# Reordering loads and DMA transposes on the queues of a four-batch attention and MLP-mixer kernel

## The chip, the cores and the metric

One core of a Trainium2 chip. The metric is the device time of one execution in microseconds (us); several executions are timed and the median is quoted. A profile is one more execution, taken by the hardware profiler. Its span is a little shorter than the timed figure of the same execution (256.6 against 258.4 us before).

The engines, as this kernel uses them: PE does the matrix products, ACT the functions such as Exp and Relu, DVE and POOL element-wise work, and SP here only issues DMA transfers (PEld is the loading of weights for PE). PSUM is where this kernel has PE put its results; an eviction is the copy of such a tile out of PSUM by ACT or DVE. The granted clock is the share of PE's full clock that it got (1.00 is full).

## The reference, cut to what matters

Four batches, eight heads, 768 positions, head dimension 64. Each query sees its window of 128 keys and the first four keys (the sinks). The attention output, as `[batch, 768, 512]`, goes through an MLP mixer.

```python
def _attn_ref(q, k, v, n_sink, window):
    scores = scale * np.matmul(q, k.transpose(0, 1, 3, 2))
    keep = is_sink | in_window              # 4 sinks, window of 128
    a = softmax(np.where(keep, scores, -1e9))       # written out in the original
    return np.matmul(a, v)

def _moe_ref(x, w_tok1, w_tok2, w_ch1, w_ch2):
    xt = x.transpose(0, 2, 1)
    h = np.maximum(xt @ w_tok1, 0.0) @ w_tok2
    u = x + h.transpose(0, 2, 1)            # token mixing
    h2 = np.maximum(u @ w_ch1, 0.0) @ w_ch2 # channel mixing
    return u + h2
```

## The kernel before

Batches run one behind the other, overlapped: while the channel layers of batch b run on PE, the attention of batch b+1 is threaded in between, and near the end the token layers of batch b+1 (its "head"). The heads of a batch form two groups of four; groups 2 and 3 belong to batch 1, 4 and 5 to batch 2, 6 and 7 to batch 3. The program order is also the order on each engine's queue: a `spread` function places each piece of the fill at a fraction of the main work.

Names used below: `x_b` is the attention output, `u` (`u_sb`) the token-mixing result, `uT` its transpose (for batches 1 to 3 by DMA transposes, six per batch, issued from the SP queue), `ps_v` the PSUM tile of the first channel layer (24 tiles a batch, evicted in turn by ACT and DVE), `ps_w` that of the second. The seam is the place where PE goes from the last `ps_w` of one batch to the first `ps_v` of the next. It needs the first three `uT`.

```python
def cast_and_turn(G, which, copy):              # q (0) or k (1) of a group
    ...
    copy(...)                                   # float32 to bf16, on POOL
    nc.sync.dma_start_transpose(out=T, in_=flat)

def utr(st):                                    # one of six transposes of u
    if b > 0:
        nc.sync.dma_start_transpose(out=uT[:, :, ts(st, P)], in_=u_sb[:, st])
        return
    ...                                         # batch 0: by PE and ACT

def ch1(half, ft):                              # first channel layer, one tile
    ...
    if ft % 2 == 0:
        nc.scalar.activation(v1[...], ps, AF.Relu)
    else:
        nc.vector.tensor_scalar(out=v1[...], in0=ps, scalar1=0.0, scalar2=None, op0=ALU.max)

def prep_v(g):
    cast_v(held[g])
    if g + 2 < NG and g >= 2:
        fetch(g + 2)                            # three loads of 768 KB from SP: q, k, v
...
seq += [build_mask0, lambda: cast_sinks(GB, NG)]   # last of the start: DVE and POOL work
run(seq)
for b in range(B):
    main, fill = mixers.pop(b)[2], []
    ...                                         # attention of batch b+1: up to fraction mid
    if b + 2 < B:
        fill += [(mid + 0.01, lambda n=n: prep_qk(n)) for n in (h + 1, h + 2)]
        fill += [(mid + 0.01, lambda n=n: prep_v(n)) for n in (h + 1, h + 2)]
    hi = mid + 0.03                             # then the head: token layers, transposes of u
    fill += [(hi + (0.97 - hi) * n / (len(nhead) - 1), f) for n, (f, _) in enumerate(nhead)]
    run(spread(main, fill))
```

The softmax here doesn't subtract the row's maximum and nothing guards it: scores larger than these inputs give would overflow.

## Time and profile before

Median 257.99 us of three runs (256.86 to 258.50). The two lines below, from the profile page of the kernel before, give 40 equal slices of the span (6.4 us each): the busy tenths of PE, and the granted PE clock in tenths of full speed.

```profile
PE   8996859997998960005888999979799999999993
PEclk9999968999999997555999999997999999999999
```

PE is nearly always busy, but for a hole in slices 16 to 18. The clock is lower at the hole (0.7 and then 0.5 in slices 16 to 19), once near 35 us (0.6) and once near 174 us (0.7). The stretches below put numbers on the stages from the first `ps_v` of batch 0 (37.48 us). The columns are the stretch, its length, busy us and instructions for each engine, the clock, the DMA share (which in this view can come out above 1, here up to 1.28, and serves to compare) and GB/s.

```profile
core 0: us, PE busy (x) PEld busy (x) DVE busy (x) ACT busy (x) POOL busy (x), PEclk, DMA share, GB/s
37.48:94.00 56.52, 53.16 (x413) 29.43 (x417) 29.43 (x65) 25.05 (x39) 29.56 (x35) 0.97 1.02 207
94.00:118.53 24.53, 0.00 (x0) 0.03 (x1) 0.66 (x1) 0.00 (x0) 0.00 (x0) 0.60 1.28 222
118.53:168.21 49.68, 47.41 (x348) 25.69 (x353) 20.85 (x47) 20.32 (x38) 23.65 (x28) 0.96 0.38 81
168.21:218.77 50.56, 47.04 (x349) 25.59 (x352) 21.54 (x48) 20.60 (x38) 15.06 (x20) 0.97 0.17 49
```

Batch 0, the hole, batch 1 and batch 2. In the hole no engine computes, and DMA has the highest share of the four (1.28). Who waited for whom, on PE (us in total, times, longest):

```profile
PE ps_v L350 <- DMA uT<-u_sb: 24.6, 1, 24.6
PE ps_v L350 <- ACT v_1341 L353: 3.3, 3, 1.9
PE ps_v L350 <- ACT v_584 L353: 2.1, 3, 0.7
```

One wait for a transpose of u is 24.6 us. Its cause is on the SP queue, shown here in order of time (start, duration of the issue, line, what):

```profile
89.36 1.64 SPq L122 DMA_TRANSPOSE kT<-kb  x1
91.06 0.98 SPq L103 DMA_DIRECT2D q_1248<-in_q_dram  x1
92.09 2.54 SPq L103 DMA_DIRECT2D k_1249<-in_k_dram  x1
94.73 3.47 SPq L135 DMA_DIRECT2D v_1252<-in_v_dram  x1
...
105.50 3.50 SPq L135 DMA_DIRECT2D v_1263<-in_v_dram  x1
109.09 3.46 SPq L371 DMA_DIRECT2D out_dram<-o  x1
112.64 2.52 SPq L340 DMA_TRANSPOSE uT<-u_sb  x2
```

Six loads of batch 3, of which four are shown, stand ahead of the transposes of u, and behind them an output store of 3.5 us. At 67.5 us, more than 7 us after SP's last issue, a load took SP 0.37 us to issue; here, one behind the other, four of the six took about 3.5 us each. An estimate from the trace sets this beside the data: 768 KB at 218 GB/s (slices 16 and 17 of the page) take 3.6 us, so SP issued about as fast as the data moved. The last u had been ready on DVE since 92.9 us.

### The profile page before, as it was taken

The page shows a single profiled execution, that of the slowest core. Times are in us where ns is not written, and L with a number is a line of the kernel's source. Part 1 is how long each engine was busy: PE and PEld are TensorE (multiplying, and loading weights), DVE is VectorE, ACT ScalarE, POOL GpSimd, SP SyncE. Part 2 cuts the span into 40 slices and gives each one's busy share as a digit, 9 for nine tenths or more (in the row PEclk, how much of TensorE's full clock was granted, in tenths as well). Part 3 has the DMA queues.
Part 4 walks back from the last instruction along what each step waited for, and adds up shares of the span by engine and source line. Part 5 has one row for each costly group of instructions (what it writes and reads, how often), then busy time and mean ns, then how long its engine had stood idle before and what let it go on. Part 6 is the DMA issues. An engine that isn't in the chain of part 4 may idle for free.

```text
span 256.6 us, 3888 instructions
## 1 busy us (share of the span) xinstructions
PE 210.2 (82%) x1547; PEld 112.7 (44%) x1565; DVE 107.0 (42%) x241; ACT 91.1 (36%) x152; POOL 91.1 (36%) x121
## 2 busy tenths in 40 slices
PE   8996859997998960005888999979799999999993
PEld 3444624554565520002445665434456644554441
DVE  5657644364746450000225473531344636333221
ACT  3794224469751000002775421065754200231100
POOL 8759322018999300000485980015654000000000
PEclk9999968999999997555999999997999999999999
DMA  6999999599499999997100149550001115401122
GB/s 231 320 195 178 233 293 260 183 210 228 94 216 229 241 212 218 218 231 160 43 0 3 41 96 191 147 143 0 3 0 43 41 43 135 111 0 43 41 82 82
DMA packets 82113, 34.88 MB, mean 136 GB/s; under 512 B 72544, under 2 KB 78432, under 8 KB 82096
## 3 DMA queue, kind: packets, MB, share of 16 engines
q1 hardware_dynamic: 76560, 26.22, 49.1%
q0 software_dynamic: 4576, 7.11, 12.6%
q10 hardware_dynamic: 960, 1.31, 1.5%
q8 instruction: 12, 0.20, 0.3%
q14 instruction: 5, 0.04, 0.1%
HBM read 26.77 MB, written 6.29 MB: 129 GB/s over the span
## 4 chain that ended last, share of the span: by engine, by line
PE 57%; SPq 12%; ACT 10%; DVE 8%; DMA 6%; POOL 3%; issue 2%; DVEq 0%; ACTq 0%; POOLq 0%
PE ps_v L350 20%; PE ps_w L362 18%; ACT pT L248 7%; SPq L103 4%; DMA v_948<-in_v_dram 4%; PE ps_s L242 3%; PE ps_u L335 3%; SPq L135 3%; PE ps_h L328 3%; DMA uT<-u_sb 2%; PE ps_warm L468 2%; SPq L122 2%; SPq L371 2%; PE ps_tr L211 2%; SPq L340 2%
## 5 line engine op out<-in xcount | busy, mean ns | idle before, releaser
L350 PE MATMUL ps_v<-uT,w_ch_104 128*128 128x384 bf16 x384 | 77.6, 338 | 31.1 <-DMA uT<-u_sb 24.6
L350 PEld LDWEIGHTS <-w_ch_104 128*128 128x128 bf16 x384 | 36.6, 100 | 62.8 <-issue 42.9
L248 ACT ACTIVATE pT<-ps_s 128x1024 bf16<-128x1024 f32 (+1 forms) x48 | 43.6, 957 | 8.5 <-PE ps_s L242 7.8
L252 POOL TENSOR_TENSOR pT<-pT,mask_92 128x512 bf16<-128x512 bf16 x12 | 13.8, 1153 | 74.8 <-ACT pT L248 74.8
L365 DVE TENSOR_TENSOR o<-ps_w,u_sb 128x512 f32<-128x512 f32 x24 | 16.6, 692 | 22.0 <-PE ps_w L362 22.0
L336 DVE TENSOR_TENSOR u_sb<-ps_u,x_b 128x512 bf16<-128x512 f32 x24 | 16.3, 687 | 18.3 <-PE ps_u L335 17.0
L259 POOL TENSOR_SCALAR_AFFINE_SELECT pT<-pT 128x640 bf16<-128x640 bf16 x24 | 18.3, 764 | 13.8 <-ACT pT L248 13.8
L355 DVE TENSOR_SCALAR v_584<-ps_v 128x384 bf16<-128x384 f32 x12 | 6.7, 557 | 38.9 <-PE ps_v L350 38.9
L353 ACT ACTIVATE v_584<-ps_v 128x384 bf16<-128x384 f32 x12 | 5.9, 494 | 42.7 <-PE ps_v L350 42.6
L293 DVE TENSOR_TENSOR x_b<-ps_o,rc 128x256 bf16<-128x256 f32 x42 | 17.8, 425 | 1.5
L362 PE MATMUL ps_w<-w_ch_105,v_584 128*128 128x512 bf16 x69 | 17.5, 379 | 0.2
L362 PE MATMUL ps_w<-w_ch_105,v_1341 128*128 128x512 bf16 x69 | 17.5, 379 | 0.2
L362 PE MATMUL ps_w<-w_ch_105,v_112 128*128 128x512 bf16 x68 | 17.3, 379 | 0.2
L242 PE MATMUL ps_s<-qT,kT 64*128 64x256 bf16 x192 | 16.0, 275 | 1.3 <-ACT pT L248 0.8
L353 ACT ACTIVATE v_1922<-ps_v 128x384 bf16<-128x384 f32 x12 | 5.9, 491 | 29.7 <-PE ps_v L350 16.2
L362 PE MATMUL ps_w<-w_ch_105,v_1922 128*128 128x512 bf16 x70 | 15.9, 379 | 0.1
L262 POOL TENSOR_SCALAR_AFFINE_SELECT pT<-pT 128x512 bf16<-128x512 bf16 x24 | 15.6, 650 | 0.0
L280 PEld LDWEIGHTS <-pT 128*128 128x128 bf16 x192 | 14.3, 98 | 2.8 <-issue 0.4
L280 PE MATMUL ps_o<-va,pT 128*128 128x65 bf16 x168 | 14.9, 194 | 0.0
L292 DVE RECIPROCAL rc<-ps_o 128x4 f32<-128x4 f32 x42 | 7.5, 179 | 17.1 <-PE ps_o L284 10.5
L328 PE MATMUL ps_h<-x_b,w_tok_102 128*128 128x256 bf16 x96 | 13.4, 272 | 1.0 <-DVE x_b L293 0.5
L353 ACT ACTIVATE v_1341<-ps_v 128x384 bf16<-128x384 f32 x12 | 5.9, 493 | 22.3 <-DVE o L365 13.4
(130 smaller groups left out, 271.6 us busy)
## 6 DMA issues: line engine op xcount, KB each, us to landing
out_dram<-o SPq DMA_DIRECT2D x23, 256.0 KB, 2.2
w_ch_104<-in_moe_w_ch_dram POOLq DMA_DIRECT2D x2, 768.0 KB, 9.3
w_ch_105<-in_moe_w_ch_dram POOLq DMA_DIRECT2D x2, 768.0 KB, 18.8
k_114<-in_k_dram ACTq DMA_DIRECT2D x2, 384.0 KB, 5.6
q_113<-in_q_dram SPq DMA_DIRECT2D x2, 384.0 KB, 4.9
q_119<-in_q_dram SPq DMA_DIRECT2D x2, 384.0 KB, 8.3
v_117<-in_v_dram SPq DMA_DIRECT2D x1, 768.0 KB, 10.6
v_123<-in_v_dram SPq DMA_DIRECT2D x1, 768.0 KB, 13.7
```

The lines of the kernel that those rows point to most:

```text
L242: nc.tensor.matmul(ps[:, i, at:at + w].rearrange("p (c q) -> p c q", q=P), G.T[1][j][ds(64 * i, 64), kt], G.T[0][j][ds(64 * i, 64), kt:kt ...
L248: nc.scalar.activation(pT[:, :, 512 * u:512 * u + n], ps[:, :, 0:n], AF.Exp, scale=scale)
L259: nc.gpsimd.affine_select(out=cur, in_=cur, compare_op=ALU.is_ge, fill=0.0, base=0, pattern=[[0, NT - 1], [1, P]], channel_multiplier=-1)
L262: nc.gpsimd.affine_select(out=prv, in_=prv, compare_op=ALU.is_ge, fill=0.0, base=-1, pattern=[[0, NT - 2], [-1, P]], channel_multiplier=1)
L280: nc.tensor.matmul(o, pT[:, i, ds(256 * qt, P)], G.va[:, h, qt], start=(qt < 2 and h == 0), stop=(h == GH - 1 and qt == 0), skip_group_che ...
L293: nc.vector.tensor_tensor(out=x_b[:, qt, c0:c0 + GH * D].rearrange("p (h d) -> p h d", h=GH), in0=o[:, :, 0:D], in1=rc.to_broadcast([P, GH ...
L328: nc.tensor.matmul(ps, w_tok1[:, t, ts(tt, P)], x_b[:, t, ds(a * GH * D, GH * D)], start=(t == 0), stop=(t == NT - 1))
L336: nc.vector.tensor_tensor(out=u_sb[:, st], in0=ps, in1=x_b[:, st], op=ALU.add)
L350: nc.tensor.matmul(ps, w_ch1[:, c, ts(ft, P)], uT[:, c, ds(half * HS, HS)], start=(c == 0), stop=(c == NC - 1))
L353: nc.scalar.activation(v1[:, ft, ds(half * HS, HS)], ps, AF.Relu)
L362: nc.tensor.matmul(ps, v1[:, ft, ts(st, P)], w_ch2[:, ft], start=(ft == 0), stop=(ft == NF - 1))
L365: nc.vector.tensor_tensor(out=o, in0=ps, in1=u_sb[:, st], op=ALU.add)
```

## The change

Its intent is to issue loads well before they are needed, at places where no DMA transpose waits behind them, and to put the q and k transposes of a batch's first group between those of u. It also clears the start of batch 0 of work for later groups. The diff, cut to its core (signatures of helpers and renamings left out):

```diff
-            ps = ps_ms.tile([P, DM], FP32, name="ps_u", tag="ms")
+            ps = (ps_mx if b == 0 else ps_ms).tile([P, DM], FP32, name="ps_u", tag="mx" if b == 0 else "ms")
...
-            m = [T2(0), T2(1), X(0), T2(2), X(1), X(2), ...
+            m = [T2(0), T2(1), T2(2), X(0), X(1), X(2), ...
...
         def prep_v(g):
             cast_v(held[g])
-            if g + 2 < NG and g >= 2:
-                fetch(g + 2)
+
+        def turn_qk(g):
+            turn(held[g], 0)
+            turn(held[g], 1)
...
-            after(load_v(held[2]), last)        # v of groups 2 and 3: SP queue
-            load_v(G)
+            load_v(held[2], nc.gpsimd)          # now POOL queue
+            load_v(G, nc.gpsimd)
...
-        seq += [lambda: cast_v(G0), lambda: cast_sinks(0, GB), step(1, 1, 2), ...
+        seq += [lambda: cast_sinks(0, GB), C(G1, 1, 0, by_pool), ...      # earlier
-        seq += [build_mask0, lambda: cast_sinks(GB, NG)]
...
                 if b == 0:
-                    order += [(lambda: prep_qk(2), 0)]
+                    fill += [(0.15, build_mask0), (0.2, lambda: cast_sinks(GB, NG))]
+                    do(prep_qk, 2)
+                    do(fetch_qk, 4)             # later in this list: fetch 5, v of 4 and 5
+                else:
+                    do(fetch_qk, h + 1)         # the six loads: start of batch 1's fill
+                    do(fetch_v, h + 1)
+                    do(fetch_qk, h + 2)
+                    do(fetch_v, h + 2)
...                                              # second group's begin and sink copies: later
-                lo, mid = (0.36, 0.80) if b == 0 else (0.02, 0.68)
+                lo, mid = (0.36, 0.80) if b == 0 else (0.06, 0.68)
...
-                hi = mid + 0.03
-                fill += [(hi + (0.97 - hi) * n / (len(nhead) - 1), f) for n, (f, _) in enumerate(nhead)]
+                hi = mid + 0.02
+                for n, (f, _) in enumerate(nhead):
+                    fill += [(hi + (0.93 - hi) * n / (len(nhead) - 1), f)]
+                    if n == 6 and nxt:          # nxt: the two groups of batch b+2
+                        fill += [(fill[-1][0], lambda n=nxt[0]: turn_qk(n))]
+                if nxt:
+                    fill += [(0.98, lambda n=nxt[1]: turn_qk(n))]
```

More of the change, by code (lines that the diff above doesn't have):

```diff
@@ L115, in cast, with flat, cast_all, turn @@
         copy(dst[:, j].rearrange("p t i d -> p i t d"), src[:, 2 * j:2 * j + 2])
-    def cast_and_turn(G, which, copy):
-        src, dst = ((G.q32, G.qb), (G.k32, G.kb))[which]
-        flat = dst.rearrange("p j t i d -> p (j t i d)")
-        copy(flat.rearrange("p (t h d) -> p t h d", t=NT, h=GH), src.rearrange("p h t d -> p t h d"))
+    def flat(G, which):
+        return (G.qb, G.kb)[which].rearrange("p j t i d -> p (j t i d)")
+    def cast_all(G, which, copy):
+        copy(flat(G, which).rearrange("p (t h d) -> p t h d", t=NT, h=GH),
+             (G.q32, G.k32)[which].rearrange("p h t d -> p t h d"))
+    def turn(G, which):
         T = att.tile([P, 2 * NT, P], BF16, name="qT" if which == 0 else "kT")
-        nc.sync.dma_start_transpose(out=T, in_=flat)
+        nc.sync.dma_start_transpose(out=T, in_=flat(G, which))
         G.T[which] = [T.rearrange("d (t j) p -> d t j p", j=2)[:, :, j] for j in range(2)]
@@ L132, in by_act, with load_v @@
         nc.scalar.activation(o, i, AF.Copy)
-    def load_v(G):
-        return nc.sync.dma_start(out=G.v32.rearrange("p h t d -> p (h t) d"),
+    def load_v(G, eng=nc.sync):
+        return eng.dma_start(out=G.v32.rearrange("p h t d -> p (h t) d"),
                                  in_=v[G.b, G.h0:G.h0 + GH].rearrange("h (t p) d -> p (h t) d", p=P))
@@ L380, in mixer @@
             hf = NF // 2
-            m = [T2(0), T2(1), X(0), T2(2), X(1), X(2), C1(0, 0), T2(3), C1(0, 1), X(3), T2(4), C1(0, 2), X(4), T2(5),
+            m = [T2(0), T2(1), T2(2), X(0), X(1), X(2), C1(0, 0), T2(3), C1(0, 1), X(3), T2(4), C1(0, 2), X(4), T2(5),
                  C1(0, 3), X(5)]
@@ L414, in start_batch, with fetch_qk, fetch_v @@
             mixers[b] = mixer(b, xs[b])
-        def fetch(g):
-            G = held[g] = tiles(g)
-            load_q(G, 0, GH)
-            load_k(G, 0, GH)
-            load_v(G)
+        def fetch_qk(g):
+            if g < NG:
+                G = held[g] = tiles(g)
+                load_q(G, 0, GH)
+                load_k(G, 0, GH)
+        def fetch_v(g):
+            if g < NG:
+                load_v(held[g])
         def prep_qk(g, by=(by_pool, by_pool)):
-            if held[g].dma:
-                for which in range(2):
-                    cast_and_turn(held[g], which, by_pool)
+            G = held[g]
+            if G.dma:
+                cast_all(G, 0, by_pool)
+                cast_all(G, 1, by_pool)
                 return
@@ L428, in prep_qk @@
                 for which in range(2):
-                    cast(held[g], j, which, by[which])
+                    cast(G, j, which, by[which])
         def prep_v(g):
             cast_v(held[g])
-            if g + 2 < NG and g >= 2:
-                fetch(g + 2)
+        def turn_qk(g):
+            turn(held[g], 0)
+            turn(held[g], 1)
         def begin(g):
@@ L487, in more_loads @@
             load_q(G, 0, GH, nc.gpsimd)
-            last = load_k(G, 0, GH, nc.gpsimd)
-            after(load_v(held[2]), last)
-            load_v(G)
+            load_k(G, 0, GH, nc.gpsimd)
+            load_v(held[2], nc.gpsimd)
+            load_v(G, nc.gpsimd)
         idle(11)
@@ L496 @@
         seq += [step(1, 0, 1), step(0, 1, 5), step(1, 1, 0)]
-        seq += [C(G1, 1, 0, by_pool), C(G1, 1, 1, by_pool), step(0, 2, 0), step(1, 0, 2), step(1, 1, 1), step(1, 0, 3)]
-        seq += [lambda: cast_v(G0), lambda: cast_sinks(0, GB), step(1, 1, 2), load_tok, step(1, 1, 3)]
+        seq += [lambda: cast_sinks(0, GB), C(G1, 1, 0, by_pool), C(G1, 1, 1, by_pool), step(0, 2, 0), step(1, 0, 2), step(1, 1, 1), step(1, 0, 3)]
+        seq += [lambda: cast_v(G0), step(1, 1, 2), load_tok, step(1, 1, 3)]
         seq += [step(0, 3, 0), step(1, 1, 4), step(0, 3, 1), lambda: cast_v(G1), step(0, 3, 2), step(1, 2, 0)]
@@ L513 @@
                 order = []
+                do = lambda f, *x: order.append((lambda: f(*x), 0))
                 if b == 0:
-                    order += [(lambda: prep_qk(2), 0)]
-                order += [(lambda g=g: begin(g), 0)] + ([(lambda h=h: begin(h), 0)] if b > 0 else [])
-                if held[g].dma:
-                    order += [(step(x, 0, i), 0) for x in (g, h) for i in range(2)]
-                else:
-                    order += [(step(g, 0, i), 8) for i in range(4)]
+                    fill += [(0.15, build_mask0), (0.2, lambda: cast_sinks(GB, NG))]
+                    do(prep_qk, 2)
+                    do(fetch_qk, 4)
+                else:
+                    do(fetch_qk, h + 1)
+                    do(fetch_v, h + 1)
+                    do(fetch_qk, h + 2)
+                    do(fetch_v, h + 2)
+                do(begin, g)
+                order += [(step(g, 0, i), 0 if held[g].dma else 8) for i in range(2 if held[g].dma else 4)]
                 for n in range(3):
@@ L524 @@
                 if b == 0:
-                    order += [(lambda: prep_qk(3, (by_dve, by_act)), 0)]
-                order += [(lambda h=h: begin(h), 0)] if b == 0 else []
-                if not held[h].dma:
-                    order += [(step(h, 0, i), 8) for i in range(4)]
-                if b == 0:
-                    order += [(lambda: prep_v(2), 0), (lambda: prep_v(3), 0)]
+                    do(prep_v, 2)
+                    do(prep_qk, 3, (by_dve, by_act))
+                    do(fetch_qk, 5)
+                    do(fetch_v, 4)
+                do(begin, h)
+                order += [(step(h, 0, i), 0 if held[h].dma else 8) for i in range(2 if held[h].dma else 4)]
                 for n in range(3):
                     order += [(step(h, 1, 2 * n), 0), (step(h, 1, 2 * n + 1), 10)]
+                    if b == 0 and n == 1:
+                        do(prep_v, 3)
+                        do(fetch_v, 5)
                     order += [(step(g, 3, 2 * n), 6), (step(g, 3, 2 * n + 1), 6)]
@@ L540 @@
                     t += w
-                if b + 2 < B:
-                    fill += [(mid + 0.01, lambda n=n: prep_qk(n)) for n in (h + 1, h + 2)]
-                    fill += [(mid + 0.01, lambda n=n: prep_v(n)) for n in (h + 1, h + 2)]
-                hi = mid + 0.03
-                fill += [(hi + (0.97 - hi) * n / (len(nhead) - 1), f) for n, (f, _) in enumerate(nhead)]
+                nxt = (h + 1, h + 2) if b + 2 < B else ()
+                fill += [(mid + 0.01, lambda n=n: prep_qk(n)) for n in nxt]
+                fill += [(mid + 0.01, lambda n=n: prep_v(n)) for n in nxt]
+                hi = mid + 0.02
[5 more added lines that the diff above has]
+                    fill += [(0.98, lambda n=nxt[1]: turn_qk(n))]
             run(spread(main, fill))
```

## The prediction

> **What bounds it now.** The one-line view of 40 slices shows PE near full except one hole. The waits give it: the first channel-mix matmuls of batch 1 (ps_v) wait 24.6 us for the DMA transpose of u, 94.0 to 118.5 us.  The SP queue's timeline shows why: its order puts six 768 KB loads of batch 3 (q, k, v of groups 6 and 7) ahead of an output store and the six u transposes; from 91.1 to 109.0 us SP issues these loads, about 3.5 us each. The transposes start at 112.6. Stages by PE: start 0-29.7, batch 0 29.7-94 (granted clock 0.77 to 44.3), hole 24.5, batch 1 49.7, batch 2 50.6, batch 3 37.8 us.
>
> **What the change does.**
> 1. SP order at the seam of batch 0 and 1 becomes: outputs, three u transposes, q/k transposes of group 4, three u transposes, q/k transposes of group 5, only then the six loads. By my count u(0..2) are issued about 6.5 us of PE work before batch 1 needs them (1.2 us to issue, 2.5 us to land, each). The six loads then run under batch 1. The hole should go: -24.5 us.
> 2. After the hole the clock was 0.5 until about 122; batch 1's mean is 0.96. [...] Without it: -1.5 us.
> 3. mask0 and the sink casts of later groups leave the DVE queue between x and u of batch 0 (29.7 to 33.1 us). The first ps_v should start at about 34.7 instead of 37.5, at a warmer clock: -4 us in total.
> 4. Batches 1 and 2: sink copies of one group (0.85 us of ACT) instead of two ahead of the first Exps, and these later (0.06, not 0.02). Before, PE waited 2.1 and 3.3 us for ACT evictions there, and in batch 2 the clock fell again (0.87, 0.91): -1 and -2 us.
> 5. Loads of groups 4 and 5 are issued earlier, as buffers come free; v of groups 2 and 3 go to the POOL queue. [...] the trace has them busy nearly all of 0-84 us, so no gain in bytes, only order. No PE time gained.
>
> **On the critical path:** items 1 to 4. 258.0 - 24.5 - 1.5 - 4 - 3 = 225.0; I add 0.5 for new frictions: **225.5 us**, range 221 to 232. Faster by over 2%: 0.97; within 2%: 0.02; slower: 0.01.
>
> **What would show it.** Step 1: no PE wait over 3 us on uT; the last loads between u stages, 20 us into batch 1; batch 1 starting right after batch 0. Step 2: no clock of 0.5 after 45 us. Step 3: first ps_v at 34-35 us. Step 4: PE waits for ACT under 2 us in each of batches 1 and 2.
>
> **What would make it wrong.** The v loads have 3072 pieces each on POOL's queue; if POOL stalls while issuing them, the casts of group 2 come late and PE stalls near 50 us (up to 5 us). q/k of group 4, now loading from about 40 us, could delay q, k of group 3 or the second weight matrix. If the PE is slower when it never rests, batches 1 and 2 would not shrink.

In item 2, "it" is the hole; the -1.5 us is an estimate, near what the trace before gives: a clock of 0.50 from 118.53 to 122.00 us is 1.7 us lost. In item 5, "them" are the core's 16 DMA engines. The 3072 pieces of a v load are its rows of 256 bytes, counted from the program.

## The result, and the profile after

Median 231.02 us of four runs (229.92 to 232.47, the last just outside the predicted range); the kernel before, in all its runs up to then, 258.25 us (256.86 to 258.67). The ratio is 0.8957, 95% interval 0.8897 to 0.9018. (A ratio is the mean time of one kernel's runs over that of the other's of the same rounds, so not quite the ratio of the medians.) Executions over 1.5% slower than the fastest of the same kernel are left out of the means. The median lies in the predicted range, 5.5 us above the predicted middle. The slices after (5.7 us each):

```profile
PE   7898868499799999788899999987999999999993
PEclk9999999979999999999999999999999999999999
```

The hole is gone. A smaller dip of PE (slice 8, near 43 us) is left, and one of the clock in the slice after it. The same stretches after are batch 0, batch 1 and batch 2, with no hole between them:

```profile
33.24:93.32 60.08, 53.32 (x413) 29.49 (x418) 33.35 (x74) 24.93 (x39) 32.46 (x39) 0.97 0.92 199
93.32:142.81 49.49, 45.75 (x349) 25.24 (x352) 21.39 (x48) 20.33 (x38) 23.81 (x28) 1.00 0.93 180
142.81:191.55 48.74, 45.97 (x349) 25.33 (x352) 21.40 (x48) 20.26 (x38) 15.04 (x20) 1.00 0.34 83
```

The SP queue at the seam, after:

```profile
87.29 3.93 SPq L344 DMA_TRANSPOSE uT<-u_sb  x3
91.32 1.43 SPq L126 DMA_TRANSPOSE qT<-qb  x1
92.84 1.80 SPq L126 DMA_TRANSPOSE kT<-kb  x1
94.74 1.52 SPq L344 DMA_TRANSPOSE uT<-u_sb  x1
...
104.36 0.92 SPq L103 DMA_DIRECT2D q<-in_q_dram  x1
```

The first three transposes of u are issued by 91.2 us; PE starts batch 1 at 93.32 us with no wait for them. The six loads follow, from 104.4 us on, and run under batch 1, whose DMA share goes from 0.38 to 0.93. The waits of PE after, the three longest:

```profile
PE ps_v L354 <- ACT v L357: 3.0, 5, 0.6
PE ps_v L354 <- DVE v L359: 2.9, 1, 2.9
PE ps_w L366 <- ACT v L357: 1.9, 2, 1.0
```

The table splits the span by the first `ps_v` of each batch, read from the trace.

| us | before | after | predicted change | measured change |
|---|---|---|---|---|
| start, to the first `ps_v` of batch 0 | 37.48 | 33.24 | (with the next line) | -4.24 |
| batch 0 and the hole | 81.05 | 60.08 | -28.5 for both | -20.97 |
| batch 1 | 49.68 | 49.49 | | -0.19 |
| batch 2 | 50.56 | 48.74 | -4.5 for both | -1.82 |
| batch 3 | 37.83 | 37.65 | 0 | -0.18 |
| span | 256.6 | 229.2 | -33, and +0.5 of friction | -27.4 |

So the hole (24.5 us) accounts for nearly all of the gain. Without the hole, batch 0 took 56.5 us before and 60.1 after: the 4.2 us won in the start were lost again in batch 0. And batches 1 and 2, with a better clock (1.00 against 0.96 and 0.97), are hardly shorter. These two were the questions for the experiments. One wait in batch 1 is new, in the same list:

```profile
PE ps_s L246 <- DMA kT<-kb: 1.2, 1, 1.2
```

Where batch 0 loses is on DVE. After, its queue between 38 and 45 us:

```profile
38.49 0.48 DVE L173 MEMSET mask<- 128x512 bf16 x1
39.98 0.48 DVE L180 MEMSET mask<- 4x512 bf16 x1 [1.00 <-POOL mask L177]
40.40 0.48 DVE L359 TENSOR_SCALAR v<-ps_v 128x384 bf16<-128x384 f32 x1
40.81 0.77 DVE L195 TENSOR_SCALAR vsink<-vs_c,dm 16x384 bf16<-16x384 f32 x1
41.50 0.79 DVE L198 CAST vsink<-dm 16x6 bf16<-16x6 f32 x1
42.20 1.05 DVE L195 TENSOR_SCALAR vsink<-vs_c,dm 16x384 bf16<-16x384 f32 x1
...
44.04 0.54 DVE L359 TENSOR_SCALAR v<-ps_v 128x384 bf16<-128x384 f32 x1
```

The eviction at 44.04 stands behind eight sink casts (`vsink`), and PE behind the eviction: that is the 2.9 us wait. The same eight casts took 1.6 us before (31.59 to 33.16; the first and the last are shown); here they take 3.3 us (40.81 to 44.13).

```profile
31.59 0.28 DVE L191 TENSOR_SCALAR vsink<-vs_c,dm 16x384 bf16<-16x384 f32 x1
33.00 0.16 DVE L194 CAST vsink<-dm 16x6 bf16<-16x6 f32 x1
```

POOL runs its casts of q and k of group 2 during the first part of that (39.78 to 43.03; two of four are shown):

```profile
40.55 0.82 POOL L133 CAST kb<-k 128x768 bf16<-128x768 f32 x1
42.21 0.82 POOL L133 CAST kb<-k 128x768 bf16<-128x768 f32 x1
```

A cast of 16x6 elements, 0.16 us before, takes 0.79 us beside the POOL casts, and 0.16 us again at 43.17 us, when they are over. By what mechanism they hold it up is not shown.

### The profile page after: what moved, and what is told of

Read it like the earlier page. It is cut to its first block, busy times and chain, and to the rows that moved or that the text cites. A ratio compares the mean times of both kernels' runs of the same rounds, so it can differ in the third digit from the quotient of the medians.

```text
span 229.2 us, 3886 instructions
## 1 busy us (share of the span) xinstructions
PE 205.5 (90%) x1547; PEld 111.3 (49%) x1565; DVE 107.0 (47%) x241; ACT 90.5 (40%) x152; POOL 93.9 (41%) x123
## 4 chain that ended last, share of the span: by engine, by line
PE 58%; DMA 13%; ACT 11%; DVE 7%; issue 5%; POOL 3%; SPq 1%; POOLq 0%; DVEq 0%
PE ps_w L366 26%; PE ps_v L354 18%; ACT pT L252 7%; DMA w_ch<-in_moe_w_ch_dram 5%; DMA v<-in_v_dram 5%; PE ps_h L332 3%; PE ps_u L339 3%; PE ps_s L246 2%; ACT v L357 2%; DVE o L369 2%; DMA k<-in_k_dram 2%; DMA kT<-kb 2%; PE ps_o L284 2%; PE ps_o L288 1%; PE ps_o L279 1%
## 5 line engine op out<-in xcount | busy, mean ns | idle before, releaser
L354 PE MATMUL ps_v<-uT,w_ch 128*128 128x384 bf16 x384 | 75.4, 331 | 7.4 <-ACT v L357 3.0
L366 PE MATMUL ps_w<-w_ch,v 128*128 128x512 bf16 x275 | 68.0, 379 | 2.7 <-ACT v L357 1.9
L357 ACT ACTIVATE v<-ps_v 128x384 bf16<-128x384 f32 x48 | 23.8, 495 | 81.7 <-PE ps_v L354 44.9
L354 PEld LDWEIGHTS <-w_ch 128*128 128x128 bf16 x384 | 35.9, 99 | 37.7 <-issue 17.8
L359 DVE TENSOR_SCALAR v<-ps_v 128x384 bf16<-128x384 f32 x48 | 26.6, 554 | 45.9 <-PE ps_v L354 45.9
L366 PEld LDWEIGHTS <-v 128*128 128x128 bf16 x288 | 27.1, 98 | 32.2 <-issue 4.2
L256 POOL TENSOR_TENSOR pT<-pT,mask 128x512 bf16<-128x512 bf16 x12 | 13.8, 1153 | 47.0 <-ACT pT L252 47.0
L284 PE MATMUL ps_o<-va,pT 128*128 128x65 bf16 x192 | 16.4, 194 | 0.0
L288 PE MATMUL ps_o<-va,pT 128*128 128x65 bf16 x160 | 14.9, 194 | 0.0
L332 PE MATMUL ps_h<-x_b,w_tok 128*128 128x256 bf16 x96 | 13.4, 272 | 1.0 <-DVE x_b L297 0.5
L339 PE MATMUL ps_u<-h,w_tok 128*128 128x512 bf16 x46 | 13.5, 379 | 0.7 <-DVE u_sb L340 0.3
```

Source lines behind the costliest of these rows:

```text
L284: nc.tensor.matmul(o, pT[:, i, ds(256 * qt, P)], G.va[:, h, qt], start=(qt < 2 and h == 0), stop=(h == GH - 1 and qt == 0), skip_group_che ...
L332: nc.tensor.matmul(ps, w_tok1[:, t, ts(tt, P)], x_b[:, t, ds(a * GH * D, GH * D)], start=(t == 0), stop=(t == NT - 1))
L339: nc.tensor.matmul(ps, w_tok2[:, tt, ts(st, P)], h1[:, tt], start=(tt == 0), stop=(tt == NTOK - 1))
L354: nc.tensor.matmul(ps, w_ch1[:, c, ts(ft, P)], uT[:, c, ds(half * HS, HS)], start=(c == 0), stop=(c == NC - 1))
L357: nc.scalar.activation(v1[:, ft, ds(half * HS, HS)], ps, AF.Relu)
L359: nc.vector.tensor_scalar(out=v1[:, ft, ds(half * HS, HS)], in0=ps, scalar1=0.0, scalar2=None, op0=ALU.max)
```

## The experiments

Each kernel was timed in five rounds with the kernel before on the same chip; the median of the kernel before was 257.27, 257.64 and 256.26 us in the three sessions (255.91 in the third without its slow run). The changed kernel was not timed again in them, so comparisons with its 231.0 us are across sessions and chips. Where a few tenths matter, the stage lengths of the trace are used, which repeat better than the totals: batch 2, which the trials with the sink casts spread or moved leave alone, takes 48.74 us in both of them and in the changed kernel. All results were correct.

### Only the order of the six loads

```diff
 def prep_v(g):
     cast_v(held[g])
-    if g + 2 < NG and g >= 2:
+    if g + 2 < NG and 2 <= g < 4:
         fetch(g + 2)
...  # after the head of b == 0
+    fill += [(0.99, lambda n=n: fetch(n)) for n in (h + 3, h + 4)]
```

> The kernel before with one thing moved: the six loads of groups 6 and 7 are issued after the six u transposes of the seam instead of ahead of them. Theory (order on the SP queue is the whole of the gain): the 24.6 us wait of ps_v on the u transpose falls under 3 us, and the time is 258 - 24 = 234 us or a little less, 232 to 236. Rival (the small moves, the interleaved q/k transposes and the earlier loads carry a good part): 240 us or more, with a wait on uT or on kT of over 5 us left at the seam.

Measured: 237.11 us (234.87 to 238.00), ratio 0.9208. The wait for uT fell from 24.6 to 4.0 us, not under 3. So moving six issues gives 20 of the 27 us, and a hole of 4.0 us stays. There the q and k transposes of both groups still stand ahead of those of u on the SP queue (the wait, and the last of these transposes and the first two of u):

```profile
PE ps_v L350 <- DMA uT<-u_sb: 4.0, 1, 4.0
86.99 1.68 SPq L122 DMA_TRANSPOSE kT<-kb  x1
89.83 2.53 SPq L340 DMA_TRANSPOSE uT<-u_sb  x2
```

The times agree: the first three u were ready on DVE by 86.7 us, but the first two transposes of u were issued at 89.8 us and the third at 93.0. The finding lies between the two expectations: the order of the loads is most of the gap. That the order of the transposes is the rest is read from this queue; it was not tried by itself.

### The start of batch 0 undone

The start lines of the diff above are put back (mask and sink casts between x and u, old order of the token layers, old PSUM pool); everything else stays as changed.

> The changed kernel with the start of batch 0 as it was: mask0 and the sink casts between x and u on the DVE queue, old order of tok2 and of the transposes, old PSUM pool. Theory (the new start gains 4 us at the first ps_v and gives all of it back when the eight sink casts sit between evictions at 41 to 44 us): within 1 us of the changed kernel, 230 to 232 us. Rival (the predicted step 3 is real, -4 us): 234 to 236 us.

Measured: 238.23 us (238.11 to 238.95), ratio 0.9264: 7 us slower than the changed kernel. My theory, that the new start is worth nothing, failed here; but so did the rival's 4 us. The waits of this kernel between 26 and 46 us show a new one (three lines of the list):

```profile
PE ps_ut L348 <- DVE u_sb L340: 10.3, 2, 9.9
DVE mask L180 <- POOL mask L177: 7.1, 1, 7.1
POOL v L139 <- DMA w_ch<-in_moe_w_ch_dram: 4.6, 2, 3.2
```

Read from the bottom: POOL, which now issues the v loads, waits for an earlier weight load before each of the two. (Why the issue of a v load waits for that load is not shown; the trace shows the waits, 4.6 us here and 4.9 us in the changed kernel.) The selects that build mask0 stand behind that on POOL, the mask's second fill behind them on DVE, u behind the fill, and PE behind u. The block of sink casts, here between the second fill and u, was slow again and took 3.6 us (36.08 to 39.69); two of its 16x6 casts took 0.79 and 0.80 us, the other two 0.16 us. The old start and the v loads on POOL do not go together.

### The start undone, and v back on the SP queue

```diff
-            load_k(G, 0, GH, nc.gpsimd)
-            load_v(held[2], nc.gpsimd)
-            load_v(G, nc.gpsimd)
+            last = load_k(G, 0, GH, nc.gpsimd)
+            after(load_v(held[2]), last)
+            load_v(G)
```

> The changed kernel with its start undone, as run before (238.2 us, u_sb late, PE waiting 9.9 us for it), and also v of groups 2 and 3 loaded from the SP queue after k of group 3, as in the kernel before. Theory (the old start and v on the POOL queue don't go together: POOL waits some 5 us to issue the v loads, mask0's selects stand behind them, and DVE with u_sb behind mask0): the 9.9 us wait falls to the 1.8 us of the kernel before, the time to about 230 us, 229 to 232, so equal to the changed kernel. Rival (the old start alone costs the 7 us): 236 us or more.

Measured: 231.89 us (229.59 to 232.78), ratio 0.8990. The wait for u is back to the 2.2 us (longest 1.8) of the kernel before, and the time to that of the changed kernel. The theory holds: the 7 us were the two parts' collision. It also means that the new start and v on POOL, taken together and with the sink casts where the change puts them, are worth nothing clear of the scatter against the old start and v on SP: 231.0 against 231.9 us, with overlapping ranges. The first `ps_v` came 4.2 us later in this profile (37.48 us), and batch 0 took 56.31 us, 3.8 less.

### The sink casts spread

```diff
-                    fill += [(0.15, build_mask0), (0.2, lambda: cast_sinks(GB, NG))]
+                    fill += [(0.12, mask0_a)]          # first fill and the two selects
+                    fill += [(0.155 + 0.037 * x, lambda x=x: cast_sinks(GB, NG, [x])) for x in range(GH)]
+                    fill += [(0.31, mask0_b)]          # second fill
```

> The changed kernel with the sink casts of the later groups spread one head at a time, every second first-layer tile, and mask0's two DVE fills apart from each other, so that no eviction waits for more than one of them. Theory: the 2.9 us wait of ps_v on DVE at 42 to 45 us goes and the clock stays at 1.00, so 3 to 4.5 us less, 226.5 to 228 us. Rival (it is the loads on the POOL queue, or data arriving late, that holds batch 0 back between 38 and 46 us): the same as the changed kernel within 1 us, the wait turning up as one on DMA or POOL.

Measured: 227.72 us (227.68 to 227.74), ratio 0.8850. Batch 0 takes 56.76 us instead of 60.08, and the mean clock from 38 to 54 us is 1.00 instead of 0.89. The theory holds: 3.3 us. The v loads are still issued from POOL in this kernel, so they are not what holds batch 0 back. Four of the eight spread casts were still slow (0.58 to 0.84 us, against 0.16 and 0.40 us for the other four), but with evictions between them the longest wait of PE for a DVE eviction is 0.9 us.

The spread of the times is telling too: 0.06 us here, 2.55 us in the changed kernel, whose four runs had mean clocks of 1.000, 0.993, 0.993 and 0.985 for 229.9, 231.0, 231.0 and 232.5 us. In the profiled run the clock was 1.00 up to the 2.9 us pause and 0.63 in the 3.4 us after it. So the pause costs its own length and, in that run, a fall of the clock; in the kernel before, a pause of 1.9 us up to 173.74 us was followed by a clock of 0.53 for 3.5 us. That the other runs differ by the same is likely from their mean clocks, but they have no trace.

### The block of sink casts, at another time

```diff
-                    fill += [(0.15, build_mask0), (0.2, lambda: cast_sinks(GB, NG))]
+                    fill += [(0.15, build_mask0), (0.3, lambda: cast_sinks(GB, NG))]
```

> The changed kernel with the eight sink casts still in one block on DVE, but at 0.30 of batch 0 instead of 0.20, when the POOL casts of group 2 (39.8 to 43.0 us) are over. Theory (two things make the 2.9 us wait: the block itself, and that its small operations are held up by the POOL casts running beside them, 3.3 us for 1.5 us of work): the block takes 1.5 us there, the wait of ps_v on DVE falls from 2.9 to about 1.0 us, no clock fall, time 228 to 229 us. Rival (only the place in the line of evictions matters, not POOL): the block takes 3 us again, wait 2.5 us or more, time 230.5 to 232.

Measured: 227.29 us (227.22 to 227.90), ratio 0.8877. The same block on DVE, now at 44.41 us (in the changed kernel POOL's casts end at 43.03 us; first, second and last cast, and the eviction behind it):

```profile
44.41 0.40 DVE L195 TENSOR_SCALAR vsink<-vs_c,dm 16x384 bf16<-16x384 f32 x1
44.73 0.16 DVE L198 CAST vsink<-dm 16x6 bf16<-16x6 f32 x1
...
45.93 0.16 DVE L198 CAST vsink<-dm 16x6 bf16<-16x6 f32 x1
46.01 0.54 DVE L359 TENSOR_SCALAR v<-ps_v 128x384 bf16<-128x384 f32 x1
```

It takes 1.7 us there, the wait of PE for a DVE eviction is gone from its list, and batch 0 takes 56.28 us. So one number in the change, 0.2 where 0.3 would do, costs 3.7 us (3.8 us in batch 0 of the traces): not the casts as such, but a block of them beside POOL's. The place among the evictions moved too; what is shown is that the block takes 3.3 us beside POOL's casts and 1.7 us at the later place, and that the short block stops nothing there.

### Evictions of the first half on DVE

```diff
-            if ft % 2 == 0:
+            if ft % 2 == 0 and not (half == 0 and 0 < b < B - 1):
                 nc.scalar.activation(v1[...], ps, AF.Relu)
```

> The changed kernel with the first-half evictions of the first channel layer in batches 1 and 2 all on DVE (in the changed kernel every second one is on ACT, queued behind 1 us Exps). Theory (the first 18 us of these batches are paced by ACT, busy 13 of 18 us and in order, so that the warmer clock only turned into waits for ACT): PE idle in these two stretches falls from 3.5 and 2.6 us to about 1 each, 3 to 4 us less in all, 227 to 228 us. Rival (PE or its clock paces them): no change within 1 us, or worse because DVE evictions are 0.07 us longer.

Measured: 229.50 us (228.00 to 229.92), ratio 0.8918. The total gain, 1.5 us, is smaller than expected and within the scatter that the sink casts make in batch 0. The stages are clear: batch 1 takes 48.35 us instead of 49.49, batch 2 takes 46.96 instead of 48.74, together 2.9 us less. The first 18 us of batches 1 and 2, first in the changed kernel, then in this one (columns as above):

```profile
93.32:111.32 18.00, 14.57 (x111) 7.74 (x110) 6.25 (x13) 12.91 (x25) 8.67 (x11) 1.00 0.99 195
142.81:160.81 18.00, 15.39 (x114) 8.12 (x113) 6.27 (x13) 12.88 (x25) 8.67 (x11) 1.00 0.58 120
```

```profile
93.36:111.36 18.00, 15.68 (x117) 8.13 (x117) 9.58 (x19) 10.32 (x19) 8.68 (x11) 1.00 0.99 194
141.71:159.71 18.00, 16.93 (x129) 8.79 (x128) 9.62 (x19) 11.42 (x21) 8.90 (x12) 1.00 0.56 115
```

With ACT at 12.9 of 18 us, PE is idle for 3.4 and 2.6 us. With evictions on DVE it is idle for 2.3 and 1.1 us, and gets more matmuls done (x). The clock is 1.00 in both. So a good part of the idle time in these stretches comes from the ACT queue, on which an eviction of 0.5 us stands behind Exps of 1 us each: in the changed kernel the eviction at 150.43 us starts when the two Exps ahead of it (148.84 us, 1.75 us) are over, and PE, which waited 0.54 us for it, goes on at 151.02 us.

### The q/k transposes earlier

```diff
+                if nxt:
+                    fill += [(mid + 0.015, lambda n=nxt[0]: turn_qk(n))]    # before the head
...
-                    if n == 6 and nxt:
-                        fill += [(fill[-1][0], lambda n=nxt[0]: turn_qk(n))]
```

> The changed kernel with the q/k transposes of the next batch's first group issued right after their casts, ahead of all six u transposes, not between the third and the fourth of them. Theory (batch 1 is 0.75 us longer than batch 2, 49.49 against 48.74, because kT lands late: PE waits 1.2 us for it at 96.9): that wait goes and batch 1 takes about 48.7 us, the time about 0.8 us less, 229.5 to 231 us. Rival (the loads running under batch 1 slow it): batch 1 stays at 49.5 us. Second rival (the transposes now hold up those of u): a wait of ps_v on uT of 1 us or more appears at a seam.

Measured: 231.08 us (228.98 to 231.66), ratio 0.8956, so no difference in the total. In the stages, the wait for kT is gone, no wait for uT came, and batch 1 takes 48.63 us instead of 49.49, as the theory had it. The profiled run lost as much in batch 0 (61.26 against 60.08 us), where its clock fell further (the 28 `ps_v` matmuls behind the pause took 7.71 us, against 6.55); that is the scatter of the sink casts again, and the totals alone would have hidden the 0.9 us.

### The parts together

> The changed kernel with both the spread sink casts and the DVE evictions. If the two losses are separate, they add: 3.3 us from the first (it came to 227.7) and about 2.9 us of stage time from the second, so 224.5 to 225.5 us. Rival (a shorter start only moves the same wait on): 226.5 us or more.

Measured for the spread casts with the DVE evictions: 225.25 us (224.66 to 226.37), ratio 0.8747; batches 0, 1 and 2 take 56.78, 48.35 and 46.96 us, each as in the kernel where its part was tried alone. The total is inside the range that the theory gave.

> Both of these and the early q/k transposes of the first group. Theory: 0.5 to 1 us below the kernel with the two alone, 223.5 to 224.5 us, PE busy share 92%. Rival (the early transposes cost as much as they gain): equal to it within 0.4 us.

Measured with the early q/k transposes as well: 223.36 us (223.32 to 223.60), ratio 0.8670. Batch 1 takes 47.00 us, like batch 2 with 46.96. The gain of the last part is 1.9 us in the medians, more than expected; 1.35 us of it is batch 1, and in the two profiles another 0.3 us is the start (33.24 against 33.56 us). PE is busy for 92% of the span. This is the best kernel with the one below, 34 us or 13% faster than the kernel before, and 7.7 us faster than the changed one.

### v back on SP, in the best kernel

The same edit as in the second kernel of the start, on top of the three parts.

> The best kernel so far (spread sink casts, DVE evictions, early q/k transposes: 223.4 us) with v of groups 2 and 3 loaded from SP after k of group 3, as in the kernel before, so that the loads of groups 4 and 5 stand behind them. Theory ([...]no load of these groups is waited for by PE: the earlier loads of the change are worth nothing by themselves): 223.4 us within 0.7. Rival (the earlier loads carry time): 225 us or more, with POOL casts of group 5 or a transpose waiting for a load near 85 us.

Measured: 223.43 us (223.22 to 223.71), ratio 0.8724 (the kernel before ran faster in that session). The theory holds: it makes no difference whether v of groups 2 and 3, and behind them the loads of groups 4 and 5, are issued earlier or not.

## Why the prediction was right or wrong, point by point

- **Item 1, the hole: right.** -24.5 us was predicted. The wait on uT is gone, batch 1 starts at 93.32 us right behind batch 0, and the loads run under batch 1. The trial of the order alone shows 20 us of it for the six loads; the 4.0 us left there are put down to the q/k transposes ahead of u, by the queue and not by a trial.
- **Item 3, the start: the step that failed.** It said "-4 us in total". The first `ps_v` did come earlier (33.24 us, even ahead of the predicted 34.7, with a clock of 1.00 up to 43 us), but I did not follow the eight sink casts and mask0 to their new place. There they ran beside POOL's casts, took 3.3 us instead of 1.6 and stopped PE for 2.9 us; batch 0 without the hole got 3.6 us longer. The term of the sum that was mis-sized is this one: predicted -4, measured -4.2 + 3.6, less than 1 us. Moving the block by a tenth of batch 0, or spreading it, gives it back (227.3 and 227.7 us).
- **About half of the 4.2 us hangs on chance in the old start.** In the profile before, one of the first sink casts (16x2 elements) took 1.45 us on DVE (19.52 to 20.97; the one before it 0.15 us), exactly beside a POOL cast of v (19.48 to 20.95), and x was complete at 29.63 us. In the trial of the order alone, whose start is the same code, these casts ended at 19.56, POOL's began at 19.46, x was complete at 27.95, and the first `ps_v` came at 35.18, 2.3 us before that of the kernel before. So about 2 us of the old start hang on a tenth of a microsecond. Of the four profiles with the old order two lost that toss, the second being the last trial of the start (1.42 us beside POOL's cast), and two won it. The change moves these casts earlier; x was complete at 27.9 to 28.3 us in all eight profiles with the move.
- **Items 2 and 4, clock and ACT in batches 1 and 2: mechanism partly right, size wrong.** I predicted -1.5 for the clock and -3 for waits. The clock did rise, from 0.96 and 0.97 to 1.00 in both batches; the fear of a PE that is slower when it never rests did not come true (PE busy in batch 1: 45.75 us after, 47.41 before). But batch 1 lost only 0.19 us and batch 2 lost 1.82, together 2.0 instead of 4.5. Nearly all that is missing is in batch 1, which was to win 2.5 us; batch 2 came close to its 2. In batch 1 PE's busy time fell by 1.7 us and its idle time grew by 1.5: what the faster PE won was lost again in waits. Of these 1.2 us is a new wait, for kT, which the prediction did not have. The waits on ACT alone were 2.2 and 2.1 us after (2.1 and 3.3 before), not under 2 in each as I had it. Trials show what each is worth: 0.9 us in batch 1 for the earlier q/k transposes, 1.1 and 1.8 us, together 2.9, for the DVE evictions.
- **Item 5, the earlier loads: right.** No gain, as the best kernel with v on SP shows. The feared stall of POOL did come (4.9 us of waiting in the changed kernel), for another reason than I gave: its two waits, 1.5 and 3.4 us, are for an earlier load, while its own two issues take 1.4 us each. In the changed kernel no PE time hangs on it; with the old start it costs 7 us. On SP, the issue of one load at 43.06 us took 14.4 us there, while loads of the POOL queue were under way.
- **The sum.** Item 3 fell 3.3 us short (together with the hole), items 2 and 4 fell 2.5 us short, the friction of 0.5 and 0.2 us in batch 3 go the other way: 5.1 us on the span, which is the 5.5 us between 225.5 and 231.0 within the scatter.

## What to carry to other kernels

A queue of DMA issues can be a chain of waits by itself (here six issues took 17.9 us of SP, and PE waited 24.6 us): look at what stands ahead of a transpose or a load on that queue, and put transfers with slack behind those without. Work taken off the critical path must be followed to its new place, and there checked against the neighbour engine that runs at that time; here one fraction in a list cost 3.7 us. When a faster engine gains nothing (here PE in batch 1: clock 0.96 to 1.00, time -0.19 us), look for the queue that now paces it, and judge small parts by stage lengths, not by totals that another stage makes noisy.
